# Load order in the first batch, PSUM bank groups and planner costs in a fused gated-linear-attention and low-rank-mixer kernel

## The chip, the cores and the metric

The kernel runs on one NeuronCore of a Trainium2 chip. The metric is device time in microseconds (us), from one launch; several runs are taken and their median is compared. The engines are TensorE (PE; its weight loads are shown as PEld), VectorE (DVE), ScalarE (ACT), GpSimd (POOL) and SyncE (SP, which here issues most DMAs). "SPq" and "ACTq" stand for the instruction queue of an engine when it issues a DMA.

## The reference

Two stages: a gated linear recurrence per head, then a mixer with a low-rank token part and a two-layer channel part.

```python
# B, H, S, D = 4, 8, 768, 48; DM = H*D = 384; rank 32; hidden 4*DM = 1536
for t in range(S):
    state = alpha[:, :, t, :, None] * state + einsum('bhd,bhe->bhde', k[:, :, t], v[:, :, t])
    y[:, :, t] = einsum('bhd,bhde->bhe', q[:, :, t], state)
x = y.transpose(0, 2, 1, 3).reshape(B, S, H * D)
h = x.transpose(0, 2, 1) @ U @ V
u = x + h.transpose(0, 2, 1)
out = u + maximum(u @ w_ch1, 0) @ w_ch2
```

Inputs and output are float32. Each of q, k, v and alpha is 4.7 MB over the four batches; the two channel weights are 2.4 MB each.

## The kernel before

**Tiling.** A sequence of 768 steps is cut into six chunks of 128 (C), and two chunks form a group (G = 2), so each batch has three groups and the whole kernel twelve. For each group, `stage_gla` does this: logarithm of alpha (`lt`, line 406, ACT), cumulative sums by matmuls with a triangle of ones (lines 419 to 426, buffer `cb`), exponentials of minus and plus the sum (`ai`, `aa`, lines 434 and 435, ACT), k times `ai` into `rk` and q times `aa` into `rq` (line 441, on DVE or POOL), the transposes of both (line 452 on TensorE, evacuated by a copy; for batches 2 and 3 by a DMA, line 462), the scores (line 481, two PSUM banks at a time), the causal mask while the scores are evacuated into `pm` (line 491 on DVE, or, where a chunk is in `split`, a plain copy on ACT, line 498, and a triangular selection on POOL, line 351), the state update (lines 513 and 523, evacuated into `st` by lines 534 and 537), and the outputs (lines 555 and 560), copied into `xb` by ACT (line 576). v is cast into `rv` first (line 311 or 309, the helper `copy`).

`stage_mix` then adds the low-rank part. In batch 0, the transposed sum is built directly in PSUM (matmuls with the identity, line 617, and the low-rank product, line 620), `xb` itself is left without the low-rank part, and line 686 adds that part to the final sum. In the other batches, the part is added to `xb` on DVE (lines 626 and 627), and the sum is then transposed, on TensorE (line 640) or by DMA (line 630). `mlp1` (line 657, with its ReLU on ACT or DVE, lines 668 and 670) and `mlp2` (line 679, with the final addition on DVE, line 688, and the store, line 689) are the channel part: 288 matmuls of 384 columns each, in all four batches.

**The order.** No engine's order is written out by hand. Each operation is handed to a planner (`Plan.add`) with an engine, a cost in ns, the buffers it reads and writes and a priority. `Plan.run` then simulates the engines: at each step it takes the operation that can start first, among those that can start together the one of lowest priority number, gives it a free buffer slot of each pool it needs, and writes the instructions down in the order found. `after=` adds a dependence for this simulation alone. What an instruction waits for on the chip follows only from the tiles that it reads and writes. `fill` puts matmuls without use (line 692) where the plan leaves TensorE idle.

**Buffers.** `io` has six fp32 slots; every load of q, k, v, alpha or a pair of weight parts takes one. PSUM has eight banks in one space. `pair` gives the recurrence of batches 1 to 3 two banks, (0,1) or (2,3); `gen` gives banks 4 or 5 to transposes and the like; `mlps` gives `mlp1` and `mlp2` any of the eight.

**Loads.** In batch 0, alpha goes out on SP (line 370) and k on ACT's queue (line 368), planned after a POOL memset of a part of an `h1t` slot that is not otherwise in use yet (line 367). q and v follow on SP in six chunks each (line 364), and then the first channel weight in three parts (line 333); all these are planned after the third logarithm (the list `gated`). The planner's priority puts the second channel weight (1.35) after batch 1's v (1.3). The weights are cast to bf16 as they arrive, by POOL, and one half part by DVE (line 342 or 345, shown as line 311).

Of the kernel before, what the change touches and what calls it, by code (L numbers as in the profile page):

```python
# [52 lines left out]
class Op:  # L53
    __slots__ = ("eng", "cost", "fn", "prio", "deps", "bufs", "n", "end", "users", "est", "i", "hold", "land", "descs", "dma", "slack")


class Plan:
# [12 lines left out]
    def add(self, eng, cost, fn, r=(), w=(), prio=0.0, after=(), kind=None, hold=450.0, land=550.0, descs=40, dma=None, slack=None):  # L70
        op = Op()
        op.eng, op.cost, op.fn, op.prio = eng, cost, fn, prio
        op.i, op.hold, op.land, op.descs = len(self.ops), hold, land, descs
        op.dma, op.slack = dma, self.SLACK if slack is None else slack
        op.deps, op.users, op.est, op.end = set(), [], 0.0, None
        for k in r:
            d = self.writer.get(k)
            if d is not None:
                op.deps.add(d)
        for k in w:  # L80
            d = self.writer.get(k)
            if d is not None:
                op.deps.add(d)
            op.deps.update(self.readers.get(k, ()))
        for k in r:
            self.readers.setdefault(k, []).append(op)
        for k in w:
            self.writer[k] = op
            self.readers[k] = []
        op.deps.update(x for x in after if x is not None)  # L90
        if kind is not None:
            if kind in self.kinds:
                op.deps.add(self.kinds[kind])
            self.kinds[kind] = op
        op.deps.discard(op)
        op.bufs = []
        for k in list(r) + list(w):
            b = k[0] if isinstance(k, tuple) else k
            if isinstance(b, Buf) and b not in op.bufs:
                op.bufs.append(b)  # L100
        for b in op.bufs:
            b.left += 1
        self.ops.append(op)
        return op

    def run(self):
# [11 lines left out]
        ring = []  # L118
        fill = self.fill[0]
        todo = len(self.ops)  # L120
        while todo:
# [42 lines left out]
            if eng == "SP":  # L164
                free = t
                for s, f, n in ring:
                    x = sum(m for s2, f2, m in ring if s2 >= s) + op.descs - RING
                    if x > 0:
                        free = max(free, s + (f - s) * min(1.0, x / n))
                clock[eng] = free + op.hold  # L170
                s = max(dma, clock[eng] + 850.0)
                dma = s + op.cost
                ring.append((s, dma, op.descs))
                del ring[:-24]
                op.end = dma + op.land
            else:
                clock[eng] = t + op.cost
                op.end = t + op.cost
                if op.dma is not None:
                    s = max(dma, clock[eng] + 850.0)  # L180
                    dma = s + op.dma
                    op.end = dma + op.land
# [6 lines left out]
            for u in op.users:  # L189
                u.n -= 1  # L190
                lat = 0.0 if u.eng == eng and eng == "PE" else self.LAT[eng]
                if u.eng == "SP":
                    lat += u.slack
                u.est = max(u.est, op.end + lat)
                if u.n == 0:
                    ready.setdefault(u.eng, []).append(u)
# [12 lines left out]
def kernel(  # L209
# [52 lines left out]
    rk_s = slots("rk", 3, [C, G, H, 64], BF16)  # L262
# [11 lines left out]
    pms = Pool(slots("pm", 4, [C, 2, HP, C], BF16))  # L274
# [4 lines left out]
    h1_s = slots("h1t", 3, [128, NJ, TW], BF16)  # L279
    dummy = h1_s[0].rearrange("p a b -> p (a b)")  # L280
    h1s = Pool(h1_s)
    outs = Pool(slots("ou", 5, [C, DM], FP32))
# [7 lines left out]
    pair = banks((0, 1), (2, 3))  # L290
# [9 lines left out]
    mlps = [banks(*[(i,) for i in s]) for s in (range(8),) * 4]  # L300
# [12 lines left out]
    def load_low_rank():  # L313
        P.add("POOL", 1000, lambda: nc.gpsimd.dma_start(u_sb, moe_U.rearrange("(c p) r -> p c r", p=128)), w=["u"], prio=1, dma=300.0, land=2500.0)
        for g in range(4):
            P.add("POOL", 1000, lambda g=g: nc.gpsimd.dma_start(vm_sb[32 * g : 32 * g + R, :], moe_V), w=[("vm", g)], prio=1, dma=100.0, land=2500.0)

    def load_big():
# [4 lines left out]
        cost = {"ACT": 830, "POOL": 830, "DVE": 470}  # L323
        for i, (src, dst) in enumerate(parts):
# [7 lines left out]
            if i < 3 or not False:  # L332
                gated.append(P.add("SP", 2100, lambda src=src, stage=stage: nc.sync.dma_start(stage(), src), w=[(t, i)], prio=0.5 if i < 3 else 1.35))
            else:
                P.add("ACT", 600, lambda src=src, stage=stage: nc.scalar.dma_start(stage(), src), w=[(t, i)], prio=90, after=[marks["w1"]], dma=2100.0)
            for hf in range(2):
                e = ((("POOL","DVE"),)+(("POOL","POOL"),)*2+(("POOL","POOL"),)*3)[i][hf]
# [7 lines left out]
                op = P.add(e, cost[e], f_cast, r=[(t, i)], w=[("w1" if i < 3 else "w2", i % 3 * 2 + hf)], prio=400 + i)  # L345
# [8 lines left out]
    dbank = [gen,gen3,gen3,gen3]  # L354

    marks = {}
    gated = []

    def load(b):
        ts = [Buf(io) for _ in range(4)]  # L360
        for n, (t, src) in enumerate(zip(ts, (alpha, k, q, v))):
            if b == 0 and n in (2, 3):
                for c in range(NC):
                    op = P.add("SP", 900, lambda t=t, src=src, c=c: nc.sync.dma_start(t()[:, :, 0:D].rearrange("p (h c) d -> p c h d", c=NC)[:, c], src[0, :, c * C : (c + 1) * C].rearrange("h p d -> p h d")), w=[(t, c)], prio=0.2 + ({2: (0, 1, 2), 3: (3, 4, 5)})[n][c // 2] / 100 + c / 1000, hold=350.0, descs=65)
                    gated.append(op)
            elif b == 0 and n == 1:
                gate = P.add("POOL", 1900 * 1.05 + 60, lambda: nc.gpsimd.memset(dummy[:, 0 : 1900], 0.0), prio=0)
                P.add("ACT", 870, lambda t=t, src=src: nc.scalar.dma_start(t()[:, :, 0:D], src[b].rearrange("h (c p) d -> p (h c) d", p=C)), w=[(t, c) for c in range(NC)], prio=0, after=[gate], dma=4100.0)
            else:
                op = P.add("SP", 4100, lambda t=t, src=src: nc.sync.dma_start(t()[:, :, 0:D], src[b].rearrange("h (c p) d -> p (h c) d", p=C)), w=[(t, c) for c in range(NC)], prio=b + n / 10, hold=800.0, descs=385, after=[marks.get("gate")])  # L370
                if b == 0 and n > 0:
                    gated.append(op)
        return ts

    def stage_gla(b, g, sprev, xb, ins):
# [8 lines left out]
        ek = ("POOL", "POOL", "DVE")[g] if first else "POOL"  # L384
        ekt = ("DVE", "ACT", "DVE")[g] if first else "ACT"
        pe = 900 + g if first else pr + 2
        eq = ("POOL", "DVE", "POOL+DVE")[g] if first else ("DVE" if b in (0,1,2) else "POOL")
        ev = ("POOL", "ACT", "DVE+ACT")[g] if first else "POOL"
        eqt = ("DVE", "ACT", "DVE+ACT")[g] if first else ("ACT" if b in (0,) else "DVE")
        split = ((1,),(1,),(1,))[g] if b in (0,) else ()  # L390
        cmul = {"POOL": 1720, "DVE": 870}
        ccpy = {"POOL": 830, "DVE": 460, "ACT": 830}
# [13 lines left out]
        op = P.add("ACT", 850, lambda: nc.scalar.activation(lt()[:, :, :, 0:D], ch(at), AF.Ln), r=chk(at), w=[lt], prio=890 if first else pr + 4)  # L406
        if first and g == 2:
            marks["gate"] = op
            for x in gated:
                x.deps.add(op)  # L410
        rv = Buf(rvs)
        for i0, n in parts:
            e = on(ev, i0)
            P.add(e, ccpy[e] * n / G + (100 if n < G else 0), lambda e=e, i0=i0, n=n: copy(e, rv()[:, i0 : i0 + n], ch(vt, i0, n)), r=chk(vt, i0, n), w=[(rv, i) for i in range(i0, i0 + n)], prio=pr + 3)
# [28 lines left out]
        for eng, dst, src, fac in ((ek, rk, kt, ai), (eq, rq, qt, aa)):  # L443
            for i0, n in parts if dst is rq else [(0, G)]:
                e = on(eng, i0)
                P.add(e, cmul[e] * n / G + (60 if n < G else 0), lambda e=e, dst=dst, src=src, fac=fac, i0=i0, n=n: f_mul(e, dst, src, fac, i0, n), r=chk(src, i0, n) + [fac], w=[(dst, i) for i in range(i0, i0 + n)], prio=pr + 2)
# [13 lines left out]
        for src, dst, eng in ((rk, kT, ekt), (rq, qT, eqt)):  # L460
            if b in (2,3):
                P.add("SP", 1000, lambda src=src, dst=dst: nc.sync.dma_start_transpose(dst().rearrange("p g e c -> p (g e) c"), src().rearrange("t g h w -> t (g h w)")), r=both(src), w=both(dst), prio=pr / 1000 - 1, hold=1250.0, land=1300.0, descs=66)
# [77 lines left out]
        em = ("DVE", "DVE", "DVE")[g] if first else "ACT"  # L540
# [37 lines left out]
        if b < 1 and c0 + G == NC:  # L578
# [7 lines left out]
    def stage_mix(b, xb, uT):  # L586
# [12 lines left out]
        if b < 1:  # L599
# [10 lines left out]
        if b in (0,):  # L610
# [13 lines left out]
        for c in range(NC):  # L624
# [3 lines left out]
            if b in (2,3):  # L628
                if c % 3 == 2:
                    P.add("SP", 1100, lambda c=c: nc.sync.dma_start_transpose(uT()[:, c - 2 : c + 1].rearrange("p c j t -> p (c j) t"), xb()[:, c - 2 : c + 1, :].rearrange("p c m -> p (c m)")), r=[(xb, c - i) for i in range(3)], w=[(uT, c // 3, j) for j in range(NCT)], prio=pr / 1000 - 1, hold=1300.0, land=1300.0, descs=66)  # L630
# [19 lines left out]
    def mlp1(b, uT, h1, tt):  # L650
        for jt in range(NJ):
# [11 lines left out]
            if b in (0,) or b in (2,3):  # L663
                need = [(uT, tt, j) for j in range(NCT)]
            for cts in ([(0,), (1,), (2,)] if b in (0,) and jt < 2 else [(0, 1, 2)]):
# [72 lines left out]
```

## Time and profile before

| | |
|---|---|
| median of 13 runs | 174.64 us (173.05 to 177.09) |
| the profiled execution's own time | 174.64 us |
| its span, first to last instruction | 172.9 us |
| TensorE busy | 157.8 us (91%), of it 15.9 us fills of line 692 |
| DVE busy | 93.1 us (54%) |
| ACT busy | 77.4 us (45%) |
| POOL busy | 53.5 us (31%) |
| read from and written to HBM | 24.08 MB and 4.72 MB |
| mean granted TensorE clock | 0.987 |

The profile is of one execution. Its span is 1.7 us shorter than the time of the run, which also holds what lies before the first and after the last instruction. In rows of instructions, the first number is the start and the second the length, in us; what stands in brackets is the idle time of the engine just before, and what ended it. Matmuls overlap, so that a row's length is longer than the step from one matmul to the next. In the rows by window, the columns are the window, its length, then for PE, PEld, DVE, ACT and POOL the busy time with the number of instructions, then the granted clock, the DMA engines' busy share and their GB/s.

### The profile page before, as it was taken

To read this page: it belongs to the slowest core of one execution; us is meant where nothing else is said; L and a number is where in the kernel's file an instruction comes from. 1 tells how busy PE (TensorE), PEld (TensorE's weight loads), DVE (VectorE), ACT (ScalarE), POOL (GpSimd) and SP (SyncE) were. 2 spreads that over 40 slices of the span, in tenths; PEclk is the share of its full clock that TensorE was granted. 3 is DMA by queue.
4 is the path that set the end of the run, shared out by engine and by line. 5 is a ranking of instruction groups with operands and counts; after the bars stand their busy time and mean duration, and the time that the engine had idled before them with its cause. 6 is when DMAs were issued, how large, how long until landed. Compare 5 with 4: busy or idle time off the path is not lost.

```text
span 172.9 us, 3994 instructions
## 1 busy us (share of the span) xinstructions
PE 157.8 (91%) x1670; PEld 101.3 (59%) x1670; DVE 93.1 (54%) x150; ACT 77.4 (45%) x137; POOL 53.5 (31%) x57
## 2 busy tenths in 40 slices
PE   5929979999997999999999999499999999999991
PEld 3725857656665656665666556366666565656650
DVE  2000399664478962864657647347757582644421
ACT  2019539658794449753344458225333311422200
POOL 8603935830617932473000006694000000000000
PEclk9997999999999999999999999999999999999998
DMA  3999999978899988999977899999601148101112
GB/s 90 314 243 188 188 206 345 347 194 248 239 246 397 342 227 248 259 256 127 244 205 216 270 267 247 246 209 171 188 4 45 45 42 235 45 2 49 64 72 91
DMA packets 58850, 33.14 MB, mean 192 GB/s; under 512 B 31440, under 2 KB 57680, under 8 KB 58832
## 3 DMA queue, kind: packets, MB, share of 16 engines
q1 hardware_dynamic: 56304, 31.46, 69.6%
q10 hardware_dynamic: 1552, 1.18, 2.4%
q0 software_dynamic: 976, 0.25, 1.4%
q8 instruction: 13, 0.21, 0.5%
q14 instruction: 5, 0.04, 0.1%
HBM read 24.08 MB, written 4.72 MB: 167 GB/s over the span
## 4 chain that ended last, share of the span: by engine, by line
PE 63%; DMA 15%; DVE 11%; ACT 4%; issue 2%; SPq 2%; POOL 0%; DVEq 0%; POOLq 0%; ACTq 0%
PE ps L657 23%; PE ps L679 21%; DMA io<-in_alpha_dram 7%; DMA io<-in_v_dram 6%; DVE rq L441 3%; DVE pm L491 3%; PE ps L481 3%; DMA qt<-rq 3%; PE ps L692 2%; PE ps L560 2%; PE ps L555 2%; PE ps L452 2%; PE ps L513 2%; SPq L689 1%; ACT kt L309 1%
## 5 line engine op out<-in xcount | busy, mean ns | idle before, releaser
L679 PE MATMUL ps<-w_sb,h1t 128*128 128x384 bf16 x288 | 55.5, 326 | 0.0
L657 PE MATMUL ps<-uT,w_sb 128*128 128x384 bf16 x288 | 52.4, 326 | 0.0
L668 ACT ACTIVATE h1t<-ps 128x384 bf16<-128x384 f32 x48 | 23.5, 491 | 37.6 <-PE ps L657 37.6
L670 DVE TENSOR_SCALAR h1t<-ps 128x384 bf16<-128x384 f32 x48 | 26.6, 556 | 23.1 <-PE ps L657 22.1
L657 PEld LDWEIGHTS <-w_sb 128*128 128x128 bf16 x288 | 27.4, 98 | 17.9 <-issue 0.3
L679 PEld LDWEIGHTS <-h1t 128*128 128x128 bf16 x288 | 26.8, 98 | 17.3 <-issue 0.3
L441 POOL TENSOR_TENSOR rk<-io,ai 128x768 bf16<-128x768 f32 x11 | 18.0, 1642 | 55.4 <-ACT ai L434 49.7
L491 DVE TENSOR_TENSOR pm<-ps,ut_ones 128x1024 bf16<-128x1024 f32 x21 | 25.5, 1222 | 8.0 <-PE ps L481 7.5
L688 DVE TENSOR_TENSOR ou<-xb,ps 128x384 f32<-128x384 bf16 x24 | 13.2, 551 | 13.1 <-PE ps L679 12.5
L692 PE MATMUL ps<-ones,ident 128*128 128x256 bf16 x96 | 15.9, 331 | 1.9 <-POOL ident masks.py:199 1.9
L406 ACT ACTIVATE lt<-io 128x768 bf16<-128x768 f32 x12 | 9.9, 844 | 14.3 <-DMA io<-in_alpha_dram 10.4
L692 PEld LDWEIGHTS <-ident 128*128 128x128 bf16 x96 | 10.9, 118 | 5.2 <-POOL ident masks.py:199 1.9
L576 ACT CAST xb<-ps 128x768 bf16<-128x768 f32 (+1 forms) x13 | 9.6, 750 | 7.6 <-PE ps L560 5.4
L627 DVE TENSOR_TENSOR xb<-xb,ps 128x384 bf16<-128x384 bf16 x18 | 9.4, 549 | 5.7 <-PE ps L626 5.6
L311 DVE COPY kt<-ps 128x1024 bf16<-128x1024 bf16 x2 | 1.4, 684 | 18.5 <-PE ps L452 18.5
L481 PE MATMUL ps<-qt,kt 48*128 48x128 bf16 x192 | 9.3, 218 | 1.8 <-DVE qt L311 1.2
L311 POOL CAST rv<-io 128x768 bf16<-128x768 f32 x10 | 9.6, 972 | 3.2 <-DMA io<-in_v_dram 3.2
L434 ACT ACTIVATE ai<-ps 128x768 bf16<-128x768 f32 x12 | 9.9, 823 | 0.9 <-PE ps L421 0.9
L435 ACT ACTIVATE aa<-ps 128x768 bf16<-128x768 f32 x12 | 9.9, 824 | 0.0
L309 ACT CAST st<-ps 128x192 bf16<-128x192 f32 x9 | 2.9, 320 | 15.6 <-PE ps L523 8.4
L311 POOL CAST w_sb<-io 128x768 bf16<-128x768 f32 x11 | 9.6, 907 | 0.0
L481 PEld LDWEIGHTS <-kt 48*128 48x128 bf16 x192 | 5.7, 94 | 4.6 <-issue 4.0
(68 smaller groups left out, 146.2 us busy)
## 6 DMA issues: line engine op xcount, KB each, us to landing
io<-in_moe_w_ch_dram SPq DMA_DIRECT2D x6, 768.0 KB, 7.9
out_dram<-ou SPq DMA_DIRECT2D x24, 192.0 KB, 2.2
io<-in_q_dram SPq DMA_DIRECT2D x6, 192.0 KB, 4.1
io<-in_v_dram SPq DMA_DIRECT2D x6, 192.0 KB, 4.0
vm_sb<-in_moe_V_dram POOLq DMA_DIRECT2D x4, 48.0 KB, 7.1
kt<-rk SPq DMA_TRANSPOSE x6, 2.8
qt<-rq SPq DMA_TRANSPOSE x6, 3.4
io<-in_alpha_dram SPq DMA_DIRECT2D x4, 0.2 KB, 11.2
```

The source lines that it names most:

```text
L311: ENG[eng].tensor_copy(dst, src)
L406: op = P.add("ACT", 850, lambda: nc.scalar.activation(lt()[:, :, :, 0:D], ch(at), AF.Ln), r=chk(at), w=[lt], prio=890 if first else pr + 4)
L434: P.add("ACT", 815, lambda: nc.scalar.activation(ai(), cb()[:, :, 0:DM], AF.Exp, scale=-1.0), r=[cb], w=[ai], prio=pe)
L441: ENG[eng].tensor_tensor(dst()[:, i0 : i0 + n, :, 0:D], ch(src, i0, n), fac()[:, i0 : i0 + n].rearrange("t g (h d) -> t g h d", d=D), op=A ...
L481: nc.tensor.matmul(s2[:, par, p, :], lhsT=kT()[o : o + D, i, p, :], rhs=qT()[o : o + D, i, p, :], start=(p == 0), stop=(p == HP - 1),)
L491: nc.vector.tensor_tensor(pmi().rearrange("t two hp c -> t (two hp) c"), sc().rearrange("p two (hp c) -> p (two hp) c", c=C), maskc.to_bro ...
L657: nc.tensor.matmul(hb()[:, 0, 0:TW], lhsT=w1_sb[:, ct, jt * 128 : (jt + 1) * 128], rhs=uT()[:, 3 * tt : 3 * tt + 3, ct, :], start=(ct == 0 ...
L668: P.add("ACT", 500, lambda jt=jt, hb=hb: nc.scalar.activation(h1()[:, jt, :], hb()[:, 0, 0:TW], AF.Relu), r=[hb], w=[(h1, jt)], prio=100)
L670: P.add("DVE", 560, lambda jt=jt, hb=hb: nc.vector.tensor_scalar_max(h1()[:, jt, :], hb()[:, 0, 0:TW], 0.0), r=[hb], w=[(h1, jt)], prio=100)
L679: nc.tensor.matmul(hb()[:, 0, 0:DM], lhsT=h1()[:, jt, (c % 3) * C : (c % 3 + 1) * C], rhs=w2_sb[:, jt, :], start=(jt == 0), stop=(jt == NJ ...
L688: P.add("DVE", 550, lambda: nc.vector.tensor_tensor(ou(), xb()[:, c, :], hb()[:, 0, 0:DM], op=ALU.add), r=[hb, (xb, c)], w=[ou], prio=100)
L692: P.fill_fn = lambda i: nc.tensor.matmul(ps[:, i, 0:256], lhsT=ident, rhs=fill_in, start=True, stop=True)
```

## The change

In batch 0, the POOL memset now writes the k tile itself, and the q tile is written by a POOL copy from the alpha tile before q is loaded; the planner's gate is that copy and not the third logarithm. The list `gated` and the dummy view are gone. `pair` may be any of four pairs of banks, and the state buffer `db` any bank. The weight parts of the second layer have priority 1.15. Batch 1's mixing takes batch 0's form. Engines are assigned anew for several operations, `split` covers other chunks, and slots of `rk`, `pm` and `ou` are changed. In the planner, operations marked `port` become dearer while the other of DVE and POOL runs one too, `late` adds to the time at which a load's users may start, and several costs are changed. `win` stays at 3.

```diff
-    __slots__ = (... "dma", "slack")
+    __slots__ = (... "dma", "slack", "port", "late")
...
+                other = {"DVE": "POOL", "POOL": "DVE"}.get(eng)
+                if op.port and last.get(other) is not None and last[other].port and clock[other] > t + 150.0:
+                    op.cost *= 1.75 if eng == "DVE" else 1.2
+                if eng in last:
+                    last[eng] = op
...
-                u.est = max(u.est, op.end + lat)
+                u.est = max(u.est, op.end + lat + op.late)
...
-    rk_s = slots("rk", 3, [C, G, H, 64], BF16)
+    rk_s = slots("rk", 4, [C, G, H, 64], BF16)
...
-    pms = Pool(slots("pm", 4, [C, 2, HP, C], BF16))
+    pms = Pool(slots("pm", 5, [C, 2, HP, C], BF16))
...
-    outs = Pool(slots("ou", 5, [C, DM], FP32))
+    outs = Pool(slots("ou", 4, [C, DM], FP32))
...
-    pair = banks((0, 1), (2, 3))
+    pair = banks(*((0, 1), (2, 3), (4, 5), (6, 7)))
...
-    dbank = [gen,gen3,gen3,gen3]
+    dbank = [pair0s]*4
...
-                gated.append(P.add("SP", 2100, ... prio=0.5 if i < 3 else 1.35))
+                P.add("SP", 2250, ... prio=0.5 if i < 3 else 1.15, after=[marks["gate"]])
...
-                e = ((("POOL","DVE"),)+(("POOL","POOL"),)*2+(("POOL","POOL"),)*3)[i][hf]
+                e = ((("POOL","POOL"),)+(("POOL","POOL"),)*2+(("POOL","POOL"),)*3)[i][hf]
...
+            if b == 0 and n == 2:
+                marks["gate"] = P.add("POOL", 36 * 48 * 1.07 + 60, lambda t=t: nc.gpsimd.tensor_copy(t()[:, 0:36, 0:D], ts[0]()[:, 0:36, 0:D]), r=[(ts[0], c) for c in range(NC)], w=[(t, c) for c in range(NC)], prio=2)
...
-                    op = P.add("SP", 900, ... hold=350.0, descs=65)
+                    op = P.add("SP", 950, ... hold=350.0, descs=65, after=[marks["gate"]], slack=0.0)
...
-                gate = P.add("POOL", 1900 * 1.05 + 60, lambda: nc.gpsimd.memset(dummy[:, 0 : 1900], 0.0), prio=0)
+                gate = P.add("POOL", 40 * 48 * 0.9, lambda t=t: nc.gpsimd.memset(t()[:, 0:40, 0:D], 0.0), w=[(t, c) for c in range(NC)], prio=0)
...
-                op = P.add("SP", 4100, ... descs=385, after=[marks.get("gate")])
+                op = P.add("SP", 4250, ... descs=385, after=[marks.get("gate")], late=(0.0, 0.0, 1500.0, 3000.0)[b])
...
-        ek = ("POOL", "POOL", "DVE")[g] if first else "POOL"
+        ek = ("DVE", "DVE", "POOL")[g] if first else "POOL"
...
-        eq = ("POOL", "DVE", "POOL+DVE")[g] if first else ("DVE" if b in (0,1,2) else "POOL")
-        ev = ("POOL", "ACT", "DVE+ACT")[g] if first else "POOL"
-        eqt = ("DVE", "ACT", "DVE+ACT")[g] if first else ("ACT" if b in (0,) else "DVE")
-        split = ((1,),(1,),(1,))[g] if b in (0,) else ()
-        cmul = {"POOL": 1720, "DVE": 870}
-        ccpy = {"POOL": 830, "DVE": 460, "ACT": 830}
+        eq = ("DVE", "POOL", "POOL+DVE")[g] if first else ("DVE" if b in (0,1,2,3) else "POOL")
+        ev = ("POOL", "ACT", "POOL+DVE")[g] if first else "POOL"
+        eqt = ("DVE", "DVE", "ACT")[g] if first else ("ACT" if b in (0,1) else "DVE")
+        split = ((1,), (0,), ())[g] if b in (0,1,2) else ()
+        cmul = {"POOL": 1640, "DVE": 900}
+        ccpy = {"POOL": 840, "DVE": 560, "ACT": 840}
...
-        if first and g == 2:
-            marks["gate"] = op
-            for x in gated:
-                x.deps.add(op)
...
-        em = ("DVE", "DVE", "DVE")[g] if first else "ACT"
+        em = ("ACT", "ACT", "ACT")[g] if first else "ACT"
...
-        if b < 1 and c0 + G == NC:
+        if b < 3 and c0 + G == NC:
...
-        if b < 1:
+        if b < 3:
             P.add("PE", mm(DM) * 1.5, lambda: f_utx(range(0, 4)), ...
...
-        if b in (0,):
+        if b in (0,1):
             for hf in range(2):
...
-            if b in (0,) or b in (2,3):
+            if b in (0,1) or b in (2,3):
                 need = [(uT, tt, j) for j in range(NCT)]
```

The multiplications (line 441), v's casts and the weight casts are the operations marked `port=True`; the DMA transposes get `late=500.0`; a low-rank load on POOL is costed at 500 and not 1000.

## The prediction, made before the run

> **What bounds the kernel now.** I read the page's forty slices first, then the chain that ended last, then the orders of SP and DVE, then busy time by windows.
>
> ```profile
> PE   5929979999997999999999999499999999999991
> DMA  3999999978899988999977899999601148101112
> ```
>
> Each digit is 4.3 us. TensorE looks busy from the start, but 96 of its matmuls (15.9 us, line 692) are warm-up fills without use. The DMA engines are full from the second slice to about 125 us. The chain shows where useful TensorE work begins:
>
> ```profile
> 0.86 11.59 DMA io<-in_alpha_dram
> 12.48 0.85 ACT lt L406
> ...
> 20.89 1.56 DVE rk L441
> 22.45 1.50 DVE rq L441
> ...
> 36.54 5.36 PE ps L657 x33
> ...
> 146.02 6.34 PE ps L657 x39
> ...
> 163.57 5.86 PE ps L679 x36
> 169.45 0.56 DVE ou L688
> ```
>
> Columns: start, length, what. Nothing can begin before alpha lands at 12.45. The first batch's recurrence ends with its last output matmul at 33.2 and line 657 begins at 36.54. From there TensorE streams: 39 matmuls in 6.34 us and 36 in 5.86 are 0.163 us each. The same per-piece rates summed over all later work (576 matmuls of lines 657 and 679: 93.7 us; the rest of batches 1 to 3: about 31) give 124.7 us of 132.9 between 36.5 and 169.45, so 8.2 us are lost there. **Two limits: a load-bound head of 36.5 us, then TensorE.**
>
> ```profile
> 0.86 0.89 SPq L370 DMA_DIRECT2D io<-in_alpha_dram  x1
> 1.81 14.28 SPq L364 DMA_DIRECT2D io<-in_q_dram  x6
> 16.13 6.00 SPq L364 DMA_DIRECT2D io<-in_v_dram  x6
> 22.18 2.33 SPq L333 DMA_DIRECT2D io<-in_moe_w_ch_dram  x3
> ...
> 45.29 5.60 SPq L333 DMA_DIRECT2D io<-in_moe_w_ch_dram  x3
> ```
>
> This is SP's own order. q went out at 1.81, and the k load on ACT's queue at 0.88, although the plan put both behind later work: a planned order is not a wait. So alpha, k and q share the DMA engines from the start (311, 317, 300 GB/s from 4 to 10 us), k lands at 10.2, and alpha, wanted first, at 12.45.
>
> **The change, part by part.**
>
> *Alpha alone.* The memset now writes k's own tile and a POOL copy from alpha writes q's, so these two loads must wait as other reloads of a tile do (SP waited 2.3 us for "POOL rk L441" before such a load). Alpha then has the engines to itself. Nearest rows: batch 3's alpha, k and q, each issued with little beside it, land 6.8, 7.0 and 6.7 us after issue. Alpha: 0.86+6.8 = 7.7, against 12.45: 4.8 earlier. Bounds 7.4 (the bytes at the 314 GB/s of 90-92 us) and 9.
>
> *k behind a memset.* 1920 fp32 elements; the row is 1900 bf16 in 1.68 us, so 1.70, from 2.58 to 4.3; at most twice that if time goes by bytes (6.0). ACT's issue then takes 0.84, and behind it on ACT waits only the first logarithm, which needs alpha anyway. k: 4.3+6.8+0.4 for alpha's tail = 11.5, which is 1.3 later than now; first needed when exp(-cum) is there, 7.7+3.4 (12.45 to 15.84 now) = 11.1. Cost 0.4 us on that multiply, which still starts at 11.6 and not at 15.93, and on DVE (0.95 us with POOL idle, 1.56 beside it) in place of POOL (1.64).
>
> *q behind a copy.* 1728 elements: POOL's cast has 768 in 0.825, so 1.86 us; lower end the memset's pace, 1.53; upper end POOL's multiply, 768 in 1.64, so 3.7. POOL is through its five DMA issues at 7.2, waits for alpha at 7.7, copies to 9.7. Behind it on POOL stands nothing before the multiply of group 2. On SP everything but alpha stands behind q's wait: 12 chunks of q and v, the weights, all later batches. Issue to flowing is about 2.1 us (0.86 to about 3), so q flows from 11.9; k's bytes end near 10.9, so the engines stand idle about 1 us. Chunks of 197 KB went at 186 to 214 GB/s between 12 and 20 us, so 1.0 us each: q complete at 18.3, the last of v at 24.3 (bounds 24 and 26.5). Now the last of v is issued at 21.4 and lands at about 25.3, so the load stream loses nothing.
>
> [...]
>
> *The rest of the head.* DVE is what works without a break now:
>
> ```profile
> 20.28 0.69 DVE L311 COPY kt<-ps 128x1024 bf16<-128x1024 bf16 x1 [18.51 <-PE ps L452]
> 25.86 2.36 DVE L491 TENSOR_TENSOR pm<-ps,ut_ones 128x1024 bf16<-128x1024 f32 x2 [0.26 <-PE ps L481]
> 31.55 1.10 DVE L311 CAST w_sb<-io 128x768 bf16<-128x768 f32 x1
> ```
>
> It starts at 20.28, after 18.51 idle, and is 9.46 of 10 us busy from 20 to 30. Batch 0 keeps about 12 us of DVE work (one more rk multiply and one more mask, without the three state copies and the weight cast), but the start moves to 11.6. Walking it with these durations, rk0, rk1, kt0, rq0 (q there at 14.5), kt2, qt0, a mask, qt1, rq2, three masks, the last mask ends at 24.6. That is where v arrives, so now v decides: cast 0.8, then 1.9 (31.36 to 33.22 now) give 27.0. The other end keeps today's 7.9 us from v's landing to the last output: 32.2. The walk is the nearer, and I add 1.0 for orders that don't fit: 28.0, **5.2 earlier than 33.2**. Line 657 starts 3.3 later as now, at 31.3. The first weights, behind v, land near 27 and take two casts of 0.83 on POOL; the DVE cast moved there costs nothing while line 657 reaches the third part only 3.9 us in; without that cover, 0.8.
>
> *Batch 1's mixing in batch 0's form.* TensorE loses 6 matmuls of line 626 (1.0) and 18 of line 640 (1.0) and gains 18 of line 617 (1.2), 6 of line 620 (1.0), 6 of line 686 (1.0): **+1.2**, on the bound engine. DVE saves 1.6, ACT 0.9, unneeded there.
>
> *w2 ahead of q1 and v1.* Now w2 goes out at 45.3 to 50.4 and its casts end at 61.4. TensorE has too little to do before: from 50.1 to 60.7 its pieces sum to 7.4 of 10.6 us, 3.2 lost. With w2 ahead, its casts end near 49 and lines 679 fill the hole; q1 and v1 slide to about 51.5 and 56 (now 46.6 and 51.2). Lines 657 and 679 of batch 0, 24.4 us with line 686, and 3.1 of batch 1's work without q last from 31.3 to 59, so that is covered. I take half: **-1.6** (bounds -3.2 and +3).
>
> *Load delays in the plan.* Batch 3 now stands still for v:
>
> ```profile
> 108.00:110.00 2.00, 0.32 (x2) 0.11 (x1) 1.26 (x3) 0.00 (x0) 0.27 (x1) 1.00 0.89 288
> 110.00:112.00 2.00, 1.39 (x22) 0.97 (x22) 0.36 (x1) 0.54 (x2) 2.00 (x2) 1.00 0.88 200
> ```
>
> The second number is TensorE's busy time; line 513 waited 2.3 us for the v cast. The plan now expects batch 3's loads 3 us later and can put other matmuls there. Half: **-1.1** (bounds -2.3 and 0).
>
> *Costed at nothing:* masks, copies and multiplies that change between DVE, ACT and POOL (ACT +7 us, DVE -6), fp32 output slots 5 to 4 (each drained in 2.2 us, one filled about every 2 at the end), extra rk and pm slots, any pair of banks. Cover: ACT is 45% and DVE 54% busy, and TensorE is at 10.00 of 10 in most later windows. Without the cover, ACT from 40 to 50 (8.80 of 10) is next, some 2 us.
>
> **Sum:** -5.2 +1.2 -1.6 -1.1 = -6.7. The profiled run took 174.64 with a span of 172.9; it is also the median. **167.9 us.**
>
> **Rivals.**
> *Given back in batch 1* (0.20). v1 to batch 1's line 594 takes 14.9 us now (51.2 to 66.1), DVE busy 9.41 of 10 in it. If that stays, it ends at 71, some 3 us after TensorE ran dry, and the hole isn't filled: 167.9+1.6+3 = 172.5. For: those loads really come later. Against: DVE's share of batch 1 falls by 2 masks, 3 copies and half the adds, some 6 us.
> *The writes don't help* (0.07). One queue alone could be slow, copy and memset at their upper ends, and the tail of 7.9 us stays: the last output at 26.5+7.9 = 34.4, 1.2 later; the other terms remain in half: 174.5. Against: batch 3's loads alone.
> *Banks* (0.15, the slower side). If recurrence and MLP collide on the eight shared banks and each of the nine later groups holds TensorE up by one mask's eviction of 1.22 us, 11 us are lost: 178.9. It decides from 0.75 us a group. For: today pairs keep to four banks. Against: the MLP already uses all eight and TensorE shows no bank wait from 60 to 80 or 120 to 160.
>
> **Numbers.** The forecast has 0.58, its own range 163.5 to 171 (head end 27.0 to 30, hole all or not filled). With the rivals: 163.5 to 175.5, leaving 0.05 below and 0.13 above. A difference under 0.5% (173.8 to 175.5) can't be told from none. Faster 0.78, same 0.07, slower 0.15.
>
> **What would show it.** First logarithm near 7.8; first q issue near 9.7; last v near 24.3; line 657 from about 31; w2's casts done by 50; no wait of line 513 for v over 1 us; span near 166.2. It is wrong if alpha still lands after 10, if line 657 starts after 33.5, or if TensorE has holes over 3 us between 45 and 75.

## The result: slower by 1.1%

| | before | changed |
|---|---|---|
| median | 175.60 us (48 runs) | 176.27 us (11 runs) |
| ratio, 95% interval | | 1.0112 (1.0074 to 1.0150) |
| span of the profiled run | 172.9 us | 174.0 us |
| first logarithm starts | 12.48 us | 7.96 us |
| first matmul of `mlp1` | 36.4 us | 34.8 us |
| mean granted clock | 0.987 | 0.970 |

The ratios here and below compare fast executions alone, those near a kernel's fastest, so that this one is not the quotient of the medians (1.004), and where few executions count as fast (3 of 12 in the first run below, 5 of 12 in the second, 2 of 6 in the seventh, 3 of 6 in the eleventh) a ratio near 1 says little.

The head, the stretch up to the first matmul of `mlp1`, did become shorter, by 1.6 us, and the end did not follow. The slices of the changed kernel's page (each digit 4.35 us):

```profile
PE   5993999899999999999992999989899999999991
PEclk9999699999999999999999579999999999999999
DMA  3997999979989896989989996999701372101122
```

There is a new "2" in TensorE's row at 91 to 96 us, and the granted clock falls right behind it. The chain that ended last, in the same form as shown for the kernel before (start, length, what):

```profile
4.37 9.72 DMA io<-in_k_dram
14.22 3.28 DVE rk L440 x2
...
34.95 5.85 PE ps L656 x36
...
91.16 4.18 DMA qt<-rq
95.48 0.61 PE ps L480 x8
...
118.23 4.28 DMA qt<-rq
...
164.66 5.86 PE ps L678 x36
170.55 0.55 DVE ou L687
```

(Lines are one off: 656, 678, 687 are 657, 679, 688 of before.) The head now waits for k, which takes 9.72 us, and later two transposes by DMA stand in the chain with more than 4 us each. Busy time by stretches, first the kernel before, then the changed one (window, length, then the busy time of PE, PEld, DVE, ACT and POOL, granted clock, DMA share, GB/s):

```profile
35.00:60.00 25.00, 23.43 (x266) 15.09 (x264) 17.68 (x27) 17.27 (x32) 11.52 (x12) 1.00 0.91 277
80.00:100.00 20.00, 19.44 (x240) 12.28 (x239) 13.10 (x20) 8.81 (x17) 0.00 (x0) 1.00 0.90 213
```

```profile
35.00:60.00 25.00, 25.00 (x211) 16.01 (x209) 12.85 (x21) 18.58 (x32) 11.20 (x11) 1.00 0.90 270
80.00:100.00 20.00, 16.85 (x223) 10.55 (x221) 10.39 (x15) 9.09 (x16) 4.72 (x6) 0.88 0.92 215
```

The hole of 50 to 60 us is filled (25.00 of 25, 1.57 us more than before), and a larger one stands between 80 and 100. Closer, in the changed kernel:

```profile
92.00:94.00 2.00, 0.39 (x12) 0.27 (x8) 1.23 (x1) 1.52 (x2) 1.09 (x1) 1.00 1.26 77
94.00:96.00 2.00, 0.52 (x8) 0.37 (x8) 0.00 (x0) 0.00 (x0) 0.00 (x0) 0.83 0.84 196
96.00:98.00 2.00, 2.00 (x36) 1.61 (x35) 1.82 (x2) 0.47 (x1) 0.00 (x0) 0.50 1.03 308
98.00:100.00 2.00, 2.00 (x22) 0.98 (x21) 0.54 (x1) 1.22 (x4) 0.00 (x0) 0.50 0.78 197
```

TensorE stands for 3.08 us (a "hole" below; it is the wait of line 480 for the qt transpose), and from 95 to 102 us it has half the clock: all windows from 96 to 102 show 0.50. It is "busy" there at about half the work: three matmuls of line 656 in a row take 1.17 us at 97.90 and 0.65 at 118.71, where the clock is 1.00.

### The profile page after: what moved, and what is told of

Read it like the earlier page. It is cut to its first block, busy times and chain, and to the rows that moved or that the text cites. A ratio compares the mean times of both kernels' runs of the same rounds, so it can differ in the third digit from the quotient of the medians.

```text
span 174.0 us, 4016 instructions
## 1 busy us (share of the span) xinstructions
PE 159.5 (92%) x1681; PEld 103.0 (59%) x1681; DVE 89.4 (51%) x142; ACT 82.9 (48%) x147; POOL 54.3 (31%) x59
## 4 chain that ended last, share of the span: by engine, by line
PE 77%; DMA 12%; DVE 3%; POOL 3%; ACT 1%; issue 1%; SPq 0%; POOLq 0%; DVEq 0%; ACTq 0%
PE ps L656 26%; PE ps L678 24%; DMA io<-in_k_dram 6%; DMA qt<-rq 5%; PE ps L480 4%; PE ps L559 3%; PE ps L451 3%; PE ps L691 3%; PE ps L554 2%; DMA uT<-xb 2%; DVE rk L440 2%; PE ps L512 2%; PE ps L619 1%; PE ps L616 1%; PE ps L418 1%; PE ps L419 1%
## 5 line engine op out<-in xcount | busy, mean ns | idle before, releaser
L678 PE MATMUL ps<-w_sb,h1t 128*128 128x384 bf16 x288 | 54.3, 326 | 0.0
L656 PE MATMUL ps<-uT,w_sb 128*128 128x384 bf16 x288 | 53.3, 328 | 0.4 <-DMA uT<-xb 0.4
L678 PEld LDWEIGHTS <-h1t 128*128 128x128 bf16 x288 | 27.5, 98 | 17.5 <-issue 0.5
L440 POOL TENSOR_TENSOR rk<-io,ai 128x768 bf16<-128x768 f32 x10 | 16.8, 1679 | 38.5 <-ACT ai L433 38.5
L490 DVE TENSOR_TENSOR pm<-ps,ut_ones 128x1024 bf16<-128x1024 f32 x18 | 21.7, 1220 | 7.8 <-PE ps L480 7.2
L316 POOL CAST rv<-io 128x768 bf16<-128x768 f32 (+1 forms) x11 | 10.3, 965 | 4.9 <-DMA io<-in_v_dram 4.9
L480 PE MATMUL ps<-qt,kt 48*128 48x128 bf16 x192 | 8.6, 224 | 3.3 <-DMA qt<-rq 3.1
L440 DVE TENSOR_TENSOR rq<-io,aa 128x768 bf16<-128x768 f32 (+1 forms) x11 | 10.7, 986 | 0.0
L356 POOL TENSOR_SCALAR_AFFINE_SELECT pm<-pm 128x1024 bf16<-128x1024 bf16 x6 | 6.5, 1092 | 12.3 <-DVE pm L490 7.3
L440 DVE TENSOR_TENSOR rk<-io,ai 128x768 bf16<-128x768 f32 x2 | 3.3, 1678 | 12.3 <-DMA io<-in_k_dram 12.3
```

What stands on the lines that cost most here:

```text
L316: ENG[eng].tensor_copy(dst, src)
L440: ENG[eng].tensor_tensor(dst()[:, i0 : i0 + n, :, 0:D], ch(src, i0, n), fac()[:, i0 : i0 + n].rearrange("t g (h d) -> t g h d", d=D), op=A ...
L480: nc.tensor.matmul(s2[:, par, p, :], lhsT=kT()[o : o + D, i, p, :], rhs=qT()[o : o + D, i, p, :], start=(p == 0), stop=(p == HP - 1),)
L490: nc.vector.tensor_tensor(pmi().rearrange("t two hp c -> t (two hp) c"), sc().rearrange("p two (hp c) -> p (two hp) c", c=C), maskc.to_bro ...
L656: nc.tensor.matmul(hb()[:, 0, 0:TW], lhsT=w1_sb[:, ct, jt * 128 : (jt + 1) * 128], rhs=uT()[:, 3 * tt : 3 * tt + 3, ct, :], start=(ct == 0 ...
L678: nc.tensor.matmul(hb()[:, 0, 0:DM], lhsT=h1()[:, jt, (c % 3) * C : (c % 3 + 1) * C], rhs=w2_sb[:, jt, :], start=(jt == 0), stop=(jt == NJ ...
```

## The experiments

Two theories were set up after the result. **Load stream**: what TensorE waits for in batches 2 and 3 are loads, and what stands behind loads on SP; these come when they come, however early the head ends. **Rivals**: the new order or the shared banks; SP's order at one place; a plan that does not know how late loads are. "The hold" is the first part of the change: k's load waits for the memset that writes its tile, and q's for the copy. In each run the kernel before was timed on the same chip, and ratios are to it. The chips differ (the kernel before had medians of 173.12, 175.44 and 174.28 us on the three used), so a difference of 1 or 2 us between profiles of different chips is not read as an effect; runs 1 to 4 share a chip, and so do 5 to 8 and 9 to 12. Where "order kept" is said, every engine's instructions stand as planned and only the edited ones differ. The start of the n-th ReLU on ACT (a row of line 668, or its like) shows how far a kernel is; they are the same instructions where the order is the same:

| us | 1st | 22nd | 23rd | 25th | 48th | last load lands |
|---|---|---|---|---|---|---|
| before | 37.4 | 98.3 | 99.3 | 117.2 | 163.2 | 109.6 |
| changed | 35.8 | 89.0 | 99.1 | 116.1 | 164.3 | 111.2 |
| changed, low-rank loads behind | 32.6 | 90.5 | 101.0 | 117.8 | 165.7 | 113.0 |
| changed, half loads | 35.5 | 89.1 | 95.4 | 110.9 | 157.8 | 101.2 |
| half loads, not held | 36.9 | 90.6 | 96.9 | 112.3 | 159.3 | 101.8 |
| half loads, low-rank loads behind | 32.0 | 87.1 | 93.4 | 108.9 | 155.8 | 98.1 |

**1. The hold alone, in the kernel before, order kept.**

```diff
-    lambda: nc.gpsimd.memset(dummy[:, 0 : 1900], 0.0)
+    lambda t=t: nc.gpsimd.memset(t()[:, 0:40, 0:D], 0.0)
...
+        if g == 3:
+            nc.gpsimd.tensor_copy(tq()[:, 0:36, 0:D], ta()[:, 0:36, 0:D])
```

> The kernel before with its planned order kept to the instruction; only the memset writes k's tile and a POOL copy from alpha, put behind the last low-rank load, writes q's. This is the hold alone, without a new plan. Theory 'the hold works, but k comes late' (k shares the engines with the low-rank loads and with q's first chunks): alpha lands near 8, k near 14, line 657 starts 1 to 2.5 us before 36.5, time 1 to 2 us less (ratio 0.99). Theory of the prediction: k near 11.5, the start 3 us or more earlier, though the old order cannot use all of it. Rival 'the 1.8 us that the changed kernel gained in its head came from the new order, not from the hold': start and time as before.

Ratio 0.9950 (0.9901 to 0.9999). In its profile alpha lands at 8.1, k at 13.4, and line 657 starts at 32.9, 3.5 us earlier than before; the hold shortens the head with the old order too. At the end no gain is shown: the medians of all executions on this chip are 173.92 us, and 173.12 for the kernel before. The last load lands at 108.3.

**2. The changed kernel without the hold, order kept** (memset and copy write scratch).

> The changed kernel with its planned order kept; memset and copy write a scratch region, so that k and q wait for nothing. If the hold is what shortens the head: alpha lands near 12.4, line 656 starts 1.5 to 3 us later (36.3 to 37.8 in place of 34.8), time 1.5 to 3 us more (ratio to before 1.02 to 1.03). Rival 'the order did it': start near 34.8, time as the changed kernel (ratio 1.011).

Ratio 1.0044 (1.0003 to 1.0086), not shown to be slower than the changed kernel, though alpha lands at 12.3 and line 656 starts only at 38.0. The head is 3.2 us longer and the ratio no higher: the first sign that the head does not decide, against what I expected of the time (1.02 to 1.03). The last load lands at 111.6 (111.2 with the hold).

**3 and 4. SP's order.** In the changed kernel two stores stand between batch 3's alpha load and five transposes. SP's rows (start, length; a length holds the time in which the issue was held up):

```profile
68.65 4.52 SPq L688 DMA_DIRECT2D out_dram<-ou  x1
73.39 0.70 SPq L375 DMA_DIRECT2D io<-in_v_dram  x1
74.19 5.02 SPq L461 DMA_TRANSPOSE kt<-rk  x1
79.66 0.75 SPq L375 DMA_DIRECT2D io<-in_alpha_dram  x1
80.50 5.07 SPq L688 DMA_DIRECT2D out_dram<-ou  x2
85.74 1.26 SPq L461 DMA_TRANSPOSE qt<-rq  x1
...
91.16 1.25 SPq L461 DMA_TRANSPOSE qt<-rq  x1
```

Each load is issued in 0.7 us, and what follows it is held 4.5 to 5 us. I took the stores to be the fault. In the edit, 269 and 284 are these two stores and 588 is the last transpose; the fourth run moves 751, the alpha load, too.

```diff
+        late = [x for x in order if getattr(x[1], "i", -1) in (269, 284)]
+        order = [x for x in order if getattr(x[1], "i", -1) not in (269, 284)]
+        at = [n for n, x in enumerate(order) if getattr(x[1], "i", -1) == 588][0] + 1
+        order[at:at] = late
         self.order = order
```

> The changed kernel with one difference: in SP's order, the two output stores that stand between batch 3's alpha load and batch 2's five last transposes are issued behind these transposes. Theory 'SP's order' (a store right behind a load holds SP for 4.6 us, the transposes come that much late, TensorE stands 3 us and then runs 3.4 us at half clock): the first of these transposes is issued near 81 in place of 85.7, the hole at 92 to 95.5 and the half clock behind it vanish, time 3.5 to 5 us less (ratio to before 0.98 to 0.99). Rival 'the transposes or the DMA engines themselves are slow there': the transpose takes the place of the store and waits 4.6 us itself, time as the changed kernel (1.011). Rival 'banks': hole and time stay whatever SP does.

> As the run before, but batch 3's alpha load too is issued behind the five transposes. Theory 'SP's order', in its wider form (a transpose behind a load waits as the store does): the transposes are issued from near 79.3, one behind the other each 1.3 us, the hole is gone, time 3.5 to 5 us less than the changed kernel, unless batch 3's loads, now 7 us later, open a hole near 110. If the run before it does not help and this one does, it is the load that blocks whatever follows it, not the store. Rival 'banks' or 'DMA engines': no change.

Ratios 1.0136 (1.0094 to 1.0179) and 1.0212 (1.0169 to 1.0254): neither helps, and **this theory fell in its narrow form**. In the third run the transpose took the store's place and was itself held 5.44 us (issued at 81.05), and the hole stayed at 92 to 95.5. In the fourth the transposes went out from 78 to 84, the hole moved to 90.5 to 94.8, and the chain there names the load that had been put behind:

```profile
85.76 6.91 DMA io<-in_alpha_dram
...
93.50 0.83 ACT lt L413
94.33 0.39 ACT h1t L671
...
94.76 1.11 PE ps L660 x3
```

Whichever of load, store and transpose went first in these three orders, the others waited. This speaks for the queue's content and against its order at this place. (The stretch at half clock, put at 3.4 us in the expectation, is 6.8 us long in the changed kernel's trace, 95.3 to 102.1; one of 3.4 us lies in its head, 16.8 to 20.2.)

**5 and 6. Half of the loads.** k, q and v of batches 1 to 3 load m = 24 of 48 row groups (heads 0 to 3), order and all compute kept; the sixth run also drops the hold.

```diff
-    ... nc.sync.dma_start(t()[:, :, 0:D], src[b].rearrange("h (c p) d -> p (h c) d", p=C))
+    ... nc.sync.dma_start(t()[:, 0:m, 0:D], src[b].rearrange("h (c p) d -> p (h c) d", p=C)[:, 0:m])
```

> The changed kernel, its order kept, but k, q and v of batches 1 to 3 load half of their rows (heads 0 to 3; the rest of a tile keeps what lay there), so these results are not the reference's. Theory 'load stream' (the head's gain is spent waiting for batches 2 and 3's loads, which land when they land, hold or no hold): loads of batches 2 and 3 land 8 us or more earlier, the holes at 92 to 96 and near 121 close, the first lateness of 5.6 us against the plan stays nearly flat to the end, time 5 to 7 us less than the changed kernel (ratio to before 0.97 to 0.98). Rival 'order or banks' (TensorE stands because of evictions, ACT or DVE, not loads): ratio as the changed kernel, 1.01, with holes in the same places.

> The run with half loads and, as in the second run, k and q of batch 0 not held; results not the reference's. Theory 'load stream': with the later loads out of the way, the 3.2 us that the hold gains at line 656 reach the end: this kernel takes 2.5 to 3.5 us more than the one with half loads and the hold (0.4 at the end of the profiles with whole loads). Rival: the difference stays under 1 us.

Ratios 0.9663 (0.9593 to 0.9734) and 0.9794 (0.9727 to 0.9861). The two ran on the same chip, and their times do not overlap: 167.06 to 169.59 us and 170.30 to 174.61. The fifth run's slices and stretch:

```profile
PE   5997898799999999999999899999999999999991
DMA  3998999989999987028888986796001743001112
```

```profile
80.00:100.00 20.00, 19.33 (x276) 12.19 (x274) 11.23 (x16) 12.50 (x23) 7.61 (x8) 1.00 0.88 198
```

The "2" and the half clock of 95 to 102 us are gone with the same order, the same banks, the same stores and transposes. In the table the 22nd ReLU starts at 89.0 and 89.1 in both kernels, the 23rd, behind the hole, at 99.1 and 95.4, the last at 164.3 and 157.8. **This shows that loads open the holes, by when they land or by holding up the transposes that share their queue and engines, and it clears banks, ACT and DVE.** Which of the two it is stays open. And with the loads out of the way the hold counts: the sixth run's head starts 1.4 us later (36.9 against 35.5) and ends 1.5 us later. I had expected 2.5 to 3.5; the head's start without the hold came out at 39.0 in the second run and at 36.9 here, so that the hold is worth 1.4 to 3.2 us at that place.

**7. Stores on ACT's queue**, in the first run's kernel, order kept.

```diff
-    nc.sync.dma_start(out[b, c * C : (c + 1) * C, :], ou())
+    nc.scalar.dma_start(out[b, c * C : (c + 1) * C, :], ou())
```

> The kernel before with the hold alone (first run), and the output stores issued on ACT's queue in place of SP's, at the same places of the order. In the first run's trace a store that follows a load holds SP for some 4.7 us, and the next load waits behind it (batch 3's alpha, k and q each land alone). Theory 'load stream': batch 3's loads land 3 to 8 us earlier, the holes near 100 to 110 shrink, time 1 to 3 us less than the first run (ratio to before 0.98 to 0.99). Rival 'ACT pays': 24 issues of 0.4 us or more on ACT and waits for stores in its order eat it: 0.995 or more.

Ratio 0.9838 (0.9731 to 0.9944), against 0.9950 (0.9901 to 0.9999) without this edit, on another chip: the intervals overlap, so the edit's own worth is not shown. Batch 3's k, q and v land at 97.3, 101.9 and 107.8 (97.9, 103.3 and 108.3 in the first run), 0.5 to 1.4 us earlier and not the 3 to 8 expected.

**8. The low-rank loads behind the copy**, in the changed kernel, order kept otherwise: POOL issues its five small loads after the copy that releases q.

> The changed kernel, its order kept, but POOL issues the five low-rank loads (976 small packets) behind the copy that releases q and not ahead of it. Theory 'k shares with the low-rank loads': k lands 1 to 2 us earlier than 14.1 and line 656 starts up to 1 us earlier than 34.8. Rival 'k shares with q's chunks alone': k at 14 as now. In both the time stays within 0.5% of the changed kernel (1.011), by the load stream.

The k load's time from issue to landing, first in the changed kernel, then here:

```profile
io<-in_k_dram ACTq DMA_DIRECT2D x1, 0.2 KB, 9.7
```

```profile
io<-in_k_dram ACTq DMA_DIRECT2D x1, 0.2 KB, 7.2
```

k lands at 11.6, and line 656 starts at 31.6, 3.2 us earlier than in the changed kernel. The time: 1.0111 (1.0040 to 1.0181), unchanged. The 23rd ReLU, at 101.0, is even 1.9 us later than in the changed kernel. A head better by 3.2 us is worth nothing here. Its trace shows where the gain went: TensorE stands 1.73 us from 81.7 for the cast of batch 2's v, which landed at 82.4, then 1.20 us from 89.8 and 2.53 us from 94.9 for transposes by DMA.

**9. A plan that knows loads to be later.**

```diff
-    late=(0.0, 0.0, 1500.0, 3000.0)[b]
+    late=(0.0, 2000.0, 4000.0, 8000.0)[b]
```

> The changed kernel with one number in the planner changed: loads of batches 1, 2, 3 are expected 2, 4 and 8 us later (now 0, 1.5 and 3), a new order for the same work. Theory 'load stream' (the plan believes batch 3's loads 7 to 11 us earlier than they land, and its fixed order then waits): the holes at 92 and 121 go, lateness against its own plan stays near 6, and the plan itself is 2 us longer, so 3 to 5 us less than the changed kernel (ratio to before 0.98 to 0.99). Rival 'nothing to put there' (TensorE has no other work while it waits, whatever the plan knows): ratio near 1.01.

Ratio 1.0083 (1.0028 to 1.0137), within the changed kernel's interval: no gain shown. TensorE is busy 16.66 of 20 us from 80 to 100, as in the changed kernel. Whether a better order could hide these loads stays open.

**10. Half loads and the low-rank loads behind the copy.**

> Half loads as in the fifth run (results not the reference's), and the low-rank loads behind the copy as in the eighth. Theory 'load stream': the 3.1 us that the eighth run won at line 656 (31.6 against 34.8), and could not keep, now reach the end: 1.5 to 3 us less than with half loads alone (ratio to before 0.95 to 0.957). Rival: no gain over 0.966.

Ratio 0.9565 (0.9521 to 0.9608), against 0.9663 (0.9593 to 0.9734); the last ReLU starts 2.0 us earlier (155.8 against 157.8). The edit that was worth nothing in the eighth run seems worth 2 of its 3.5 us here; the chips differ and the intervals overlap, so the fifth and sixth runs, on one chip, are the firmer pair.

**11 and 12. Three repairs in the kernel before.** The kernel before with three edits, its order kept: the hold, the low-rank loads behind the copy, the stores on ACT's queue; and the same with a new plan that expects batch 3's loads 8 us later.

> The kernel before with its order kept and three repairs: the hold, the low-rank loads behind the copy, the stores on ACT's queue. Theory 'load stream': the third repair is worth up to 1% (seventh run, 0.984), the first two together make line 657 start near 31 and yet add little at the end, since batch 3's loads stay where they are: 0.98 to 0.99. Rival 'the head counts': 2.5 us more than the seventh run, 0.97.

> The run with three repairs, and the planner told that batch 3's loads come 8 us later (a new order). Theory 'load stream': the hole of 2.3 us before batch 3's v goes, 1 to 3 us less than the run with three repairs (0.965 to 0.98). Rival 'nothing to put there': as that run or slower.

Ratios 0.9808 (0.9752 to 0.9864) and 0.9846 (0.9793 to 0.9898). Both intervals lie below 1; between the two runs no difference is shown, so that the twelfth missed its expectation. Of the kernel before, no execution on that chip was under 173.50 us. In the twelfth run five of six were (170.77 to 173.39, median of all 172.02, beside 174.28); in the eleventh three of six (170.68 to 171.40), while three took 174.41 to 176.25, so that its gain is less sure.

## Why the prediction was wrong

**Alpha, memset, copy, q: right.** Alpha lands at 7.94 (7.7 said; the lower bound of 7.4 does not follow from the 314 GB/s and the 2.1 us from issue to flowing that the step on q uses, which give 6.7), the memset takes 1.70 (1.70), the copy 1.62 (1.86), q's first chunk is issued at 9.65 (9.7).

**k: wrong by 2.6 us, and so the head.** "4.3+6.8+0.4 for alpha's tail = 11.5"; it landed at 14.1. The step left out the five low-rank loads that POOL issues just then. With these moved away, k lands at 11.6, and line 656 starts at 31.6, where 31.3 was said (eighth run). So -5.2 was really -1.6 (34.8 against 36.4; the prediction's 36.54 is the chain's first piece of line 657, and its first matmul starts at 36.37), and the rest of the walk held up. The prediction's own sign of being wrong, line 657 after 33.5, came true. The last chunk of v landed at 25.5 and not at 24.3.

**The hole of 50 to 60 us: right.** "-1.6"; TensorE's busy time from 35 to 60 rose by 1.57, and the second channel weight had landed at 48.1 in place of 58.4. q1 and v1 slid to 53.0 and 57.6 (51.5 and 56 said). By busy time the hole was 1.57 us in all; the prediction got there as half of 3.2 reckoned by piece rates, the half was a guess, and its closeness is luck.

**The step that failed is the sum itself**: "Two limits: a load-bound head of 36.5 us, then TensorE". That TensorE is busy from 36 us on in both pages hid that it stops wherever the next load is late, and those loads form one stream from 3 to 110 us that the head's edits do not touch. The last load, first before (start and time to landing), then changed (its issue, and its time to landing):

```profile
99.16 10.43 DMA io<-in_v_dram
```

```profile
103.89 1.16 SPq L375 DMA_DIRECT2D io<-in_v_dram  x1
io<-in_v_dram SPq DMA_DIRECT2D x1, 0.2 KB, 7.3
```

It lands at 109.6 before and at 111.2 changed. Two sums over the traces show why this matters. From 36 to 112 us SP's rows follow one another almost without a break: the gaps over 0.15 us between them add up to 3.0 us before, 0.5 changed and 0.5 in the eighth run, but to 17.4 with half loads. SP's queue thus does not wait for the compute that a shorter head brings forward. And in all eleven profiles with whole loads the span ends 62 to 64 us after the last load lands, whether the first matmul of `mlp1` starts at 31.6 or at 38.0. (With half loads it ends 66 to 67.5 us after it, so there the last load alone does not decide.) The prediction itself said that "the load stream loses nothing" by the hold; it did not ask whether the stream gains anything. So neither the head's 1.6 us nor the hole's 1.6 reached the end. They were lost again in a hole of 3.1 us at 92 and the slow clock behind it; the changed kernel was 9.2 us ahead at the 22nd ReLU (orders differ, so this is rough) and 1.1 us behind at the 48th. The runs show it by the same edits with whole and with half loads: leaving out the hold makes the head 3.2 us longer with whole loads, and no later end is shown (second run), but 1.4 us longer with half loads, and the end comes 1.5 us later (sixth); moving the low-rank loads makes the head 3.2 and 3.5 us shorter and gives nothing with whole loads (eighth), about 2 us with half (tenth).

**"-1.1" for batch 3's v:** the old wait (2.3 us) is gone from its place, but waits of 3.1 us (line 480) and 1.1 us (line 554) for transposes took over. **"+1.2" for batch 1's mixing** was not measured alone.

**The rivals.** "Given back in batch 1" had the mechanism, loads that come later and TensorE dry, but in batch 1 and at 172.5 us; it happened in batches 2 and 3. (Its "9.41 of 10" for DVE is the window of 50 to 60 us; from 51.2 to 66.1 DVE is busy 11.65 of 14.9.) The loads' own rows would have told: batch 3's alpha, k, q and v land 5 to 6 us after one another in the kernel before (93.3, 99.1, 104.7 and 109.6). "The writes don't help" fell with alpha at 7.94; its 174.5 halves the hole and v's wait but leaves out the +1.2 (with half of that it is 175.1). "Banks" is refuted as the cause by the half loads, which left every bank as it was.

## What to carry to other kernels

An early stage's gain reaches the end only if nothing later runs on a clock of its own: look at whether the load queue ever waits for compute and at when the last load lands, before and after, and do not count on a gain at the end that moves neither. To test it, keep the order and halve the loads; if the time falls and the early gain reappears, the stream is the bound. Before holding a load back for another, list every DMA that will then flow in the freed time.

## What the runs showed of the hardware that was not expected

- Five low-rank loads, 0.25 MB in 976 packets on queue 0, cost k's load of 1.2 MB 2.5 us (9.7 against 7.2 us from issue to landing). Over all profiles with the hold it is 8.5 to 9.7 us with them ahead (seven) and 7.0 to 7.3 with them behind (four).
- In the rows of the changed kernel and of the third run, what followed a whole load on SP's queue at once was held 4 us or more whatever it was: stores 4.52 and 4.60, transposes 5.02 and 5.44, a load 4.10; the issue of a load that did not have to wait took 0.7. Behind half a load it was 3.10 (a load) and 3.43 (a store, fifth run).
- After TensorE had stood for 3.08 us in the changed kernel (92.4 to 95.5), the granted clock was 0.50 for 6.8 us (95.3 to 102.1). After a hole of 2.3 us in the kernel before (108.3 to 110.6) it stayed at 1.00, but in the eighth run one of 2.53 us went with 6.8 us at 0.50 (95.9 to 102.7) and in the ninth one of 2.75 us with 3.4 (96.9 to 100.3), so in these four traces the length of the hole alone does not tell how long the clock stays down.
- In the changed kernel's head DVE and POOL multiply side by side (line 440, fp32 in, 128x768). DVE's took 0.96 and 0.94 us where they had begun before POOL's, and 2.40 where POOL's was already running; POOL's took 2.02 and 2.34 us in place of 1.64.
